# Raw centroids turned first, inverse norms spread by a product, first loads on one queue, and a new order of the early work

## The chip, the cores and the metric

The kernel runs on one core of a Trainium2 chip. The metric is the device time of one execution in microseconds. The kernel before takes 226.15 us as the median of three runs (226.10 to 226.18). Five engines work side by side, each through its own list of instructions in order: TensorE (PE, with its weight loads as PEld), VectorE (DVE), ScalarE (ACT), GpSimd (POOL) and SyncE (SP), which here only issues transfers. An instruction that waits holds up all that stands behind it on its engine.

## The reference, cut to what matters

```python
c_n = centroids / (norm(centroids, axis=-1) + 1e-06)        # 8 heads x 16 centroids x 64
q_assign = argmax(einsum('bhsd,hcd->bhsc', q_n, c_n), axis=-1)   # same for k
mask = q_assign[:, :, :, None] == k_assign[:, :, None, :]
scores = where(mask, scale * q @ k.T, -1e9)                  # 4 batches x 8 heads x 768 x 768
attn = softmax(scores);  x = attn @ v                        # then (3072, 512)
h = x @ w_in                                                 # 512 -> 1024
ln = layer_norm(h * softmax(h)) * g_ln
out = ln @ w_out                                             # 1024 -> 512
```

Each query row and key row gets the centroid of its head with the largest product. The mask lets a query see only keys with the same centroid. Only the direction of a centroid row counts, so each of the 128 rows (8 heads by 16) is divided by its norm.

## The kernel before, in words

A batch and two heads make a pair; there are 16 pairs. For each pair the kernel loads q and k (`raw`), turns them so that the 64 features lie on partitions (`xt`), multiplies them by the centroids on PE (`csc`, name `cl`), turns the result back on DVE (`cst`, `tb`), takes the maximum (`mx`), marks it (`oh`), turns the marks (`oht`, `ot`) and places them (`pl`) as 16 more rows under the cast features (`ca`) in the tile `qk`. One PE product over 80 or 96 rows (`S`, tile `sps`) then gives score and mask together. ACT takes exponentials (`E`, tile `e`), PE multiplies them by v (`V`, tile `ops`), DVE divides (`N`). The second half of the model runs in blocks of 128 rows: product with w_in (`h`), maximum (`hm`), exponential (`ex`), product (`u`), statistics (`bn`, `ag`, `al`), turn (`tu`), product with w_out (`y`), scale (`sc`) and store (`ou`).

The program is written by a weaver: every piece of work has a name, and five strings in `ORDER` say in which order the names stand on each engine. `AWAY` moves single pieces to another engine than their usual one. `add` gives a piece its function and what it needs; the costs there only order the writing of the program. On PE the names `wm` and `fl` stand for idle products on zeros (`idle_p`, line 854), which keep the engine at work until real work arrives. The first pair is done in two halves, one for each head (`halves_of`): q and k of head 0, then of head 1. `tp` turns a half on PE (line 402), `xa` copies it out of PSUM (line 409).

The centroids: SyncE issues their load first (line 841). DVE sums squares (line 877), POOL takes the root (line 880), DVE refines and inverts it (lines 882 to 889) and writes the scaled rows twice side by side (`c_n`, line 890). PE turns them (`cp`, line 899), DVE multiplies by a 0/1 mask `own` into `c_by_two` (`cf`, line 903), which the first five pairs use. Later PE turns them again (`cq`) and DVE writes `c_bd` (`cb`, line 910), which the other pairs use.

Tokens keep PSUM areas apart: `take="m"` and `give="m"` share one bank between `cp`, `cq`, `cl` and `y`.

Of the kernel before, what the change touches and what calls it, by code (L numbers as in the profile page):

```python
# [22 lines left out]
class Weave:  # L23
# [6 lines left out]
        ld4 lv si ld6 lv ld lg lv ld2 lo2 lv lo ld2 lo ld6 li4 tx ld lv ld6 lv tx lv tu ld5 lv ld tx  # L30
        ld tu ld tu ld8 ou ld tu ou ld4 lv ld7 lv ld tu ld4 ou tx ld tu ld4 ou tx ld5 ou ld tu ld2
        lv ld tu ld tx ld4 ou ld3 ou pl ld5 tu lv ld4 lv tu ou tu ld3 lv ou tx ld lv tu ld2 pl ou tx
        ld2 ou pl tu ou lv tx tu pl ou tu2 tx2 tu ou tx2 tu ou tu ou tx tu ou tu ou tu ou6
    """
    ORDER["POOL"] = """
        zo po =ca0.0.0.1.0 ca =pl0.0.0.1.1 pl cv =ca0.1.0.1 =ca0.1.0.0 =pl0.0.1.0.0 pl z
        =pl0.0.1.0.1 ca pl ca =cv0.1.1 =ca0.2.1.1 pl =ca0.2.0.1 pl2 ca2 =ca0.3.1.1 cv =pl0.2.0.0
        =ca0.3.1.0 cv pl =ca0.3.0.1 z pl =cv0.3.1 =ca1.0.0.0 cv =ca1.0.1.0 pl =z4 gs z ca =pl1.0.1.1
        sg ca =pl1.0.0.1 pl2 wi4 =ca1.1.1.0 =cv1.0.1 =ca1.1.0.1 cv =ca1.1.1.1 =at1 =ca1.2.0.1 at ca
        al =pl1.1.1.1 cv =pl1.1.0.0 pl bl pl ca z =ca1.2.1.1 al at ca cv =pl1.2.1.1 =pl1.2.0.0 al  # L40
        =pl1.2.0.1 pl =ca2.0.1.0 bl cv =ca1.3.0.1 at =cv1.3.1 =ca1.3.1.0 ca al =pl1.3.1.1 =pl1.3.0.0
        pl cv bl pl =cv2.1.0 ca =pl2.0.0.0 pl =at5 pl2 at al =ca2.0.1.1 =ca2.1.0.0 =pl2.1.0.1
        =ca2.1.1.1 ca cv al =ca2.3.0.0 bl cv =pl2.1.1.1 =ca2.2.0.1 =ca2.1.1.0 =pl2.1.0.0 =ca2.2.0.0
        pl bl =ca2.3.1.1 at2 al =ca2.2.1.0 cv ca cv pl =ca2.3.1.0 pl at pl =pl2.3.1.1 =pl2.3.1.0 ca
        pl at pl al =ca3.0.0.0 ca =ca3.0.1.0 bl ca =cv2.3.1 al =ca3.1.1.1 cv =pl3.0.0.0 =pl3.0.1.1
        pl bl =ca3.2.0.1 al ca =cv3.0.1 cv pl at2 ca al =pl3.1.1.1 =ca3.3.0.0 =ca3.2.0.0 =cv3.1.1
        =pl3.2.0.1 al =pl3.1.0.1 pl =ca3.2.1.0 =cv3.2.1 pl =ca3.3.0.1 cv ca cv at =ca3.3.1.0 pl cv
        al ca at =pl3.3.0.1 at =pl3.3.1.1 al pl ca =at17 at al2 at al at al =at21 at al2 =at22 at
        al3 at al
    """  # L50
    ORDER["PE"] = """
        wm fl2 tp fl2 tp fl8 cp tp fl7 cl tp fl11 cl fl16 tp S tp S cq S2 tp S tp2 S V S tp V S tp
        cl V S tp2 S V S2 V tp S V S gt tp S2 cl S2 V2 S V S tp S V S V S tp S V S cl S2 V S V3 S2
        tp2 S V S V2 S tp S V S2 cl S V S V2 S2 V S su S3 V4 S3 su S V S2 V S V2 S2 me S2 V2 S2 V2
        S2 cl S2 V S V S V2 h S3 h S h S h S V S V3 S2 h V h V S2 V S h S V S h S2 V S V h S V h S3
        V3 y2 S y S h2 S h V y S2 V2 S h cl V S2 h V h S3 h S V y S y3 V S2 V S V h V S h S V S V S
        y S h y S3 V y S V S V2 S y S V2 S2 cl h V S h S2 h V S V S2 y V S V2 S2 y S2 y2 S V h V S V
        S2 V2 S V cl S2 V2 S cl S V2 S2 y S V S V S y S V S y S V S2 y S V S V2 h V S h S h2 S y4 S
        V S h2 S V S h2 S V S V cl V h S h S V S2 cl S h S h V S2 V h S V2 h y2 S2 y2 S2 V2 S h S2 h
# [129 lines left out]
def kernel(  # L189
# [461 lines left out]
    def values(n, j):  # L651
# [4 lines left out]
        if s == 0:  # L656
            opss[g] = ps_o.tile([P, 6, VS], F32, name="ops")
# [638 lines left out]
```

## Time and profile before

| | us |
|---|---|
| median of 3 runs | 226.15 (226.10 to 226.18) |
| profiled execution, its own time | 227.3 |
| span of that execution (first to last instruction) | 225.3 |
| PE busy | 219.2 (97%) |
| DVE busy | 200.3 (89%) |
| ACT busy | 191.3 (85%) |
| POOL busy | 127.7 (57%) |

The profiled execution is 2.0 us longer than its span and 1.15 us longer than the median. Busy time of PE counts the time in which a product is in flight. The granted clock of PE is 1.0 throughout, yet idle products of one shape take different times early and late, which the chain of waits shows. In the forty equal slices of the span PE is at 9 tenths in all but the first and the last.

### The profile page before, as it was taken

How to read it: one execution, taken by the hardware profiler on the slowest of the kernel's cores; microseconds unless marked ns; L12 is line 12 of the kernel's file. 1: busy time of each engine (PE TensorE's matmuls, PEld its weight loads, DVE VectorE, ACT ScalarE, POOL GpSimd, SP SyncE). 2: the span in 40 equal slices, each digit the busy share in tenths (PEclk: the TensorE clock that was granted, in tenths of full speed). 3: DMA queues.
4: the chain of work that ended last, by engine and by line, in shares of the span. 5: the costliest groups of instructions: out<-in, count | busy, mean ns of one | idle time of the engine just before them, and what ended most of it. 6: DMA issues, size and time to landing. Idle time of an engine off the chain costs nothing.

```text
span 225.3 us, 6745 instructions
## 1 busy us (share of the span) xinstructions
PE 219.2 (97%) x2501; PEld 146.8 (65%) x2501; DVE 200.3 (89%) x359; ACT 191.3 (85%) x366; POOL 127.7 (57%) x246
## 2 busy tenths in 40 slices
PE   8999999999999999999999999999999999999993
PEld 8877864666666767666566656676666677665452
DVE  2799997899999999999999899898998996879982
ACT  3399988999979999998989979899989899964353
POOL 3379985942385597289995670957965102122341
PEclk9999999999999999999999999999999999999999
DMA  5999994289999999799997998789771724659522
GB/s 182 366 370 354 196 243 191 47 163 220 187 179 153 213 179 169 148 161 175 184 219 155 147 215 149 180 170 162 175 166 58 93 28 116 90 155 177 166 83 103
DMA packets 117327, 38.80 MB, mean 172 GB/s; under 512 B 105640, under 2 KB 112816, under 8 KB 117296
## 3 DMA queue, kind: packets, MB, share of 16 engines
q1 hardware_dynamic: 117008, 38.06, 79.0%
q8 instruction: 19, 0.31, 0.6%
q10 hardware_dynamic: 288, 0.33, 0.4%
q14 instruction: 12, 0.10, 0.2%
HBM read 23.11 MB, written 6.29 MB: 130 GB/s over the span
## 4 chain that ended last, share of the span: by engine, by line
PE 80%; DVE 10%; ACT 2%; POOL 2%; issue 2%; DMA 1%; SPq 1%; DVEq 0%; ACTq 0%; POOLq 0%
PE sps L637 23%; PE hreg L746 16%; PE yps L810 16%; PE ops L660 12%; PE hreg L402 3%; PE csc L476 3%; PE idle_p L854 3%; DVE xt L427 2%; ACT e L643 2%; PE csc L471 1%; DMA raw<-in_q_dram 1%; DVE nmax L752 1%; DVE y L827 1%; DVE oh L510 1%; PE hreg L609 1%
## 5 line engine op out<-in xcount | busy, mean ns | idle before, releaser
L643 ACT ACTIVATE e<-sps 128x512 bf16<-128x512 f32 x288 | 150.6, 610 | 10.5 <-PE sps L637 8.6
L637 PE MATMUL sps<-qk 80*128 80x256 bf16 (+3 forms) x648 | 98.9, 260 | 0.3
L637 PEld LDWEIGHTS <-qk 80*128 80x128 bf16 (+1 forms) x648 | 52.1, 97 | 32.0 <-issue 8.6
L660 PEld LDWEIGHTS <-e 128*128 128x128 bf16 x1152 | 52.5, 97 | 16.0 <-issue 4.0
L660 PE MATMUL ops<-v,e 128*128 128x65 bf16 x1152 | 58.7, 193 | 0.5 <-DVE x L685 0.3
L746 PE MATMUL hreg<-w_in_sb,xT 128*128 128x512 bf16 x192 | 54.4, 379 | 0.0
L810 PE MATMUL yps<-w_out_c,uT 128*128 128x512 bf16 x184 | 49.9, 379 | 0.3 <-DVE y L827 0.3
L765 DVE TENSOR_TENSOR u<-e_sb,hreg 128x1024 bf16<-128x1024 bf16 (+1 forms) x25 | 29.1, 1166 | 5.0 <-ACT e_sb L758 4.9
L758 ACT ACTIVATE e_sb<-hreg,nmax 128x1024 bf16<-128x1024 f32 x24 | 26.8, 1118 | 6.7 <-DVE nmax L752 6.5
L776 DVE BATCH_NORM_STATS2 bs<-u 128x6 f32<-128x512 bf16 x48 | 31.6, 676 | 0.3
L550 POOL COPY qk<-oht 32x384 f32<-32x384 f32 x40 | 20.6, 515 | 18.8 <-DVE oht L523 14.9
L752 DVE TENSOR_REDUCE nmax<-hreg 128x1 f32<-128x1024 f32 x24 | 28.9, 1203 | 1.3 <-PE hreg L746 1.1
L456 POOL CAST qk<-xt 64x768 bf16<-64x768 f32 (+1 forms) x31 | 25.5, 823 | 6.9 <-DVE xt L409 3.0
L458 POOL TENSOR_SCALAR qk<-xt 64x768 bf16<-64x768 f32 (+1 forms) x28 | 23.4, 836 | 4.0 <-PE yps L810 2.3
L810 PEld LDWEIGHTS <-uT 128*128 128x128 bf16 x200 | 17.8, 97 | 11.5 <-ACT uT L742 0.8
L746 PEld LDWEIGHTS <-xT 128*128 128x128 bf16 x192 | 16.5, 97 | 8.1 <-issue 0.6
L792 POOL TENSOR_SCALAR esq<-es,mv 128x1 f32<-128x1 f32 x24 | 8.1, 339 | 22.6 <-DVE mv L780 22.0
L427 DVE STREAM_TRANSPOSE xt<-raw 128x768 f32<-128x768 f32 x22 | 20.9, 959 | 0.0
L685 DVE TENSOR_TENSOR x<-ops,den 128x256 bf16<-128x256 f32 (+1 forms) x39 | 18.9, 486 | 1.3
L786 POOL TENSOR_SCALAR es<-esum 128x1 f32<-128x1 f32 x24 | 5.6, 239 | 23.3 <-ACT e_sb L758 14.9
L568 POOL CAST v<-vf 128x384 bf16<-128x384 f32 x27 | 14.3, 532 | 7.7 <-DMA vf<-in_v_dram 4.7
L795 POOL TENSOR_TENSOR alpha<-esq,halves 128x1 f32<-128x1 f32 x24 | 13.4, 560 | 2.0
(82 smaller groups left out, 186.6 us busy)
## 6 DMA issues: line engine op xcount, KB each, us to landing
vf<-in_v_dram SPq DMA_DIRECT2D x16, 384.0 KB, 4.4
out_dram<-y SPq DMA_DIRECT2D x23, 256.0 KB, 2.8
raw<-in_q_dram SPq DMA_DIRECT2D x44, 96.0 KB, 3.2
raw<-in_k_dram SPq DMA_DIRECT2D x44, 96.0 KB, 3.4
w_g<-in_moe_w_out_dram SPq DMA_DIRECT2D x4, 512.0 KB, 8.0
w_st<-in_moe_w_in_dram SPq DMA_DIRECT2D x4, 512.0 KB, 6.9
raw<-in_q_dram SPq DMA_DIRECT2D x4, 384.0 KB, 7.2
raw<-in_k_dram SPq DMA_DIRECT2D x4, 384.0 KB, 7.8
```

The costliest lines, as they stand in the source:

```text
L427: nc.vector.transpose(xt[:], raws[b, p, i][:].rearrange("p j c -> p (j c)"))
L456: VEC[e].tensor_copy(dst, src)
L458: VEC[e].tensor_scalar(dst, src, scalar1=inv_C, scalar2=1.0, op0=Alu.mult, op1=Alu.mult)
L637: nc.tensor.matmul(sps_[n, k][:, c0:c0 + w], side(b, h // 2, 1, h % 2, keys)[r], side(b, h // 2, 0, h % 2, slice(s0 * P, s0 * P + w))[r])
L643: nc.scalar.activation(es[n, k][:, :w], sps_[n, k][:, :w], Act.Exp, scale=exp_scale, bias=-exp_scale)
L660: nc.tensor.matmul(opss[g][:, s, :VW], es[n, k][:, c0:c0 + P], v1[slot(b, h // 2)][:, h % 2, kt, :VW], start=(kt == 0), stop=(kt == n_t - 1))
L746: uses(nc.tensor.matmul(hreg[:, at(f, f2)[1], :], xTs[f][:, dc, :], w_in_sb[:, dc, f2 * FF2:(f2 + 1) * FF2], start=(dc == 0), stop=(dc == ...
L752: uses(nc.vector.tensor_reduce(ff[f, "nmax"][:], pair_of(f), axis=AXY, op=Alu.max, negate=True), *both(f))
L758: uses(nc.scalar.activation(ff[f, "e"][:], pair_of(f), Act.Exp, bias=ff[f, "nmax"][:], accum_out=ff[f, "esum"][:]), *both(f))
L765: uses(nc.vector.tensor_tensor(ff[f, "u"][:, at_], ff[f, "e"][:, at_], pair_of(f)[:, at_], op=Alu.mult), *banks)
L776: nc.vector.bn_stats(ff[f, "bs"][:, f2, :], ff[f, "u"][:, f2, :])
L810: ins = nc.tensor.matmul(dst, ff[f, "uT"][:, at(f, f2)[0] * (n_fc // 2) + c, :], w_out_c[:, fc, cols], start=(fc == chunks[0]), stop=(fc = ...
```

## The change

The load of the centroids is issued twice, by SyncE and by ACT, into the two halves of `c_two`. PE turns these raw rows as its first real work (`cp`), ACT copies the turned rows to SBUF (`ct`, tile `c_t`). Squares, root and inverse go on meanwhile; the formula for the norm is written with one step of another kind (`c_s1`). When the inverse norms `c_inv` are there, PE multiplies them, repeated over 128 columns, by the identity (`ci`): this puts the inverse of each centroid in its column on all rows of PSUM. DVE then multiplies turned rows and inverses straight into place, in six small products: `cg` for the first pair, `cf` for the other heads of `c_by_two`, `cb` for `c_bd`. POOL clears those two tiles first and no longer makes `own`. The PSUM bank is that of `ops`, so the first `V` now needs `cf` and `cb`, and `cq` is gone.

The first load of q, which ACT issued, is issued by SyncE. In the first pair ACT copies all four turned halves (`xa`) and places one of the marks (`pl0.0.0.1.0`). The five orders are written anew from end to end, with 53 idle products in place of 72.

```diff
@@ -27,67 +27,64 @@
     ORDER["PE"] = """
-        wm fl2 tp fl2 tp fl8 cp tp fl7 cl tp fl11 cl fl16 tp S tp S cq S2 tp S tp2 S V S tp V S tp
+        wm cp fl10 tp2 ci tp fl2 cl tp fl9 cl fl14 tp S2 tp S tp S2 tp2 S2 tp cl tp S V2 S2 tp S tp
...
     AWAY.update(dict.fromkeys("""
-        ca0.0.0.0.0 ca0.0.0.1.1 ca1.3.1.1 sc23.0 tu22.1 tu23.1 xa0.0.1.0 xa0.2.1.0 xa0.2.1.1
-        xa0.3.0.0
+        ca0.0.0.0.0 ca0.0.0.1.1 ca1.3.1.1 sc23.0 tu22.1 tu23.1 pl0.0.0.1.0 xa0.0.0.1 xa0.0.1.0
+        xa0.2.1.0 xa0.2.1.1 xa0.3.0.0
     """.split(), "ACT"))
...
-            opss[g] = ps_o.tile([P, 6, VS], F32, name="ops")
+            opss[g] = ps_o.tile([P, 6, VS], F32, name="ops", tag="ops")
...
-    c_all = const.tile([P, D], F32, name="c_all")
-    nc.sync.dma_start(out=c_all[:], in_=centroids.rearrange("h c d -> (h c) d"))
+    c_two = const.tile([P, 2, D], F32, name="c_two")
+    for x, e in enumerate((nc.sync, nc.scalar)):
+        e.dma_start(out=c_two[:, x, :], in_=centroids.rearrange("h c d -> (h c) d"))
     for hh in range(2):
         for i in range(2):
-            load_head(0, 0, i, hh, nc.sync if i or hh else nc.scalar)
+            load_head(0, 0, i, hh, nc.sync)
...
-    own = const.tile([P, 2 * NC_], F32, name="own")
-    for hh in range(2):
-        for x in range(2):
-            nc.gpsimd.memset(own[hh * D:(hh + 1) * D, x * NC_:(x + 1) * NC_], float(hh == x))
+    nc.gpsimd.memset(c_by_two, 0.0)
+    nc.gpsimd.memset(c_bd[:], 0.0)
...
     c_r0 = const.tile([P, 1], F32, name="c_r0")
     nc.vector.reciprocal(c_r0[:], c_s0[:])
-    nc.vector.scalar_tensor_tensor(out=c_r0[:], in0=c_r0[:], scalar=c_nsq[:], in1=c_s0[:],
+    c_s1 = const.tile([P, 1], F32, name="c_s1")
+    nc.vector.tensor_scalar(c_s1[:], c_s0[:], scalar1=2e-6, scalar2=None, op0=Alu.add)
+    c_norm = const.tile([P, 1], F32, name="c_norm")
+    nc.vector.scalar_tensor_tensor(out=c_norm[:], in0=c_r0[:], scalar=c_nsq[:], in1=c_s1[:],
                                    op0=Alu.mult, op1=Alu.add)
-    c_norm = const.tile([P, 1], F32, name="c_norm")
-    nc.vector.tensor_scalar(c_norm[:], c_r0[:], scalar1=0.5, scalar2=1e-6,
-                            op0=Alu.mult, op1=Alu.add)
     c_inv = const.tile([P, 1], F32, name="c_inv")
     nc.vector.reciprocal(c_inv[:], c_norm[:])
-    nc.vector.tensor_scalar(c_n[:], c_all[:].unsqueeze(1).to_broadcast([P, 2, D]),
-                            scalar1=c_inv[:], scalar2=None, op0=Alu.mult)
-    add("wm", "PE", 3.55, -1000, lambda e: [idle(P) for _ in range(26)])
+    add("wm", "PE", 3.55, -1000, lambda e: [idle(P) for _ in range(18)])
...
+    def turn_centroids():
+        cs["t"] = ps_o.tile([P, 2, P], F32, name="cps", tag="ops")
+        nc.tensor.transpose(cs["t"][:, 0, :], c_two[:].rearrange("p a d -> p (a d)"), ident_f[:])
+
+    c_t = const.tile([P, P], F32, name="c_t")
+
+    def spread_inverse():
+
+        nc.tensor.matmul(cs["t"][:, 1, :], c_inv[:].to_broadcast([P, P]), ident_f[:])
+
+    def keep_blocks(dst, lo, hi, step):
+
+        for x in range(2):
+            r = slice(x * D, (x + 1) * D)
+            src = [y.rearrange("p (h c) -> p h c", c=NC_) for y in (c_t[r], cs["t"][r, 1, :])]
+            hs = slice(lo + (x if step == 2 else 0), hi, step)
+            nc.vector.tensor_tensor(dst[r, :, x * NC_:(x + 1) * NC_], src[0][:, hs], src[1][:, hs],
+                                    op=Alu.mult)
+
+    add("wa", "ACT", 2.75, -1000, lambda e: None)
+    add("cp", "PE", 0.42, 0, lambda e: turn_centroids(), [])
+    add("ct", "ACT", 0.3, -600, lambda e: nc.scalar.copy(c_t[:], cs["t"][:, 0, :]), ["cp", "wa"])
+    add("ci", "PE", 0.42, 0, lambda e: spread_inverse(), ["cn", "cp"])
+    add("cg", "DVE", 0.25, -500, lambda e: keep_blocks(c_by_two[:, 0:2], 0, 2, 1), ["ci", "ct"])
+    add("cf", "DVE", 0.3, -490, lambda e: keep_blocks(c_by_two[:, 2:H], 2, H, 1), ["ci", "ct"])
+    add("cb", "DVE", 0.3, -480, lambda e: keep_blocks(c_bd[:], 0, H, 2), ["ci", "ct"])
...
+                if n == 0:
+                    nd += ["cf", "cb"]
                 add(f"V{n}.{j}", "PE", 0.193, t_to[n] - 1 + j + 0.5,
                     (lambda e, n=n, j=j: values(n, j)), nd, [prev] if prev else [])
```

Three places show what moved. The first is the head of DVE's list, from the norms to the first marks. Before, with line numbers of the kernel before:

```order
L882 RECIPROCAL c_r_153<-c_s_151 128x1
L883 SCALAR_TENSOR_TENSOR c_r_153<-c_r_153,c_nsq,c_s_151 128x1
L886 TENSOR_SCALAR c_norm<-c_r_153 128x1
L889 RECIPROCAL c_inv<-c_norm 128x1
L890 TENSOR_SCALAR c_n<-c_all,c_inv 128x128
L458 TENSOR_SCALAR qk_99<-xt 64x3x128
L903 TENSOR_TENSOR w_out_c<-cps,own 128x256
L409 COPY xt<-hreg 128x384
L485 STREAM_TRANSPOSE cst<-csc 128x192
```

And now (`c_by_two` lies inside the tile `w_out_c`):

```order
L881 RECIPROCAL c_r_151<-c_s_149 128x1
L883 TENSOR_SCALAR c_s_153<-c_s_149 128x1
L885 SCALAR_TENSOR_TENSOR c_norm<-c_r_151,c_nsq,c_s_153 128x1
L888 RECIPROCAL c_inv<-c_norm 128x1
L910 TENSOR_TENSOR w_out_c<-c_t,cps 64x2x16 x2
L455 TENSOR_SCALAR qk_99<-xt 64x3x128
L482 STREAM_TRANSPOSE cst<-csc 128x192
```

The scaling of the rows and the copy of a turned half are gone from here, and the product over 128x256 became two over 64x2x16, ahead of the cast.

The second place is DVE's list behind the first half, up to `c_bd`. Before:

```order
L409 COPY xt<-hreg 128x384
L498 TENSOR_REDUCE mx<-cst 128x12
L910 TENSOR_TENSOR c_bd<-cps,own 128x128
L568 CAST v_0_105<-vf 128x6x64
L504 TENSOR_TENSOR w_out_c<-cst,mx 128x6x2x16
```

And now, from the cast of v on:

```order
L567 CAST v_0_105<-vf 128x6x64
L482 STREAM_TRANSPOSE cst<-csc 128x192
L406 COPY xt<-hreg 128x384
L495 TENSOR_REDUCE mx<-cst 128x12
L910 TENSOR_TENSOR w_out_c<-c_t,cps 64x6x16 x2
L406 COPY xt<-hreg 128x384 x2
L501 TENSOR_TENSOR w_out_c<-cst,mx 128x6x2x16
L517 STREAM_TRANSPOSE oht<-w_out_c 128x384
L910 TENSOR_TENSOR c_bd<-c_t,cps 64x4x16 x2
```

`c_bd` stood ahead of the marks of the second half and of three copies; it now stands behind the marks, their turn and five copies (one each after the marks and after the turn).

The third place is the end of DVE's list, the last block. Before:

```order
L740 COPY uT<-utp 128x512
L776 BN_STATS bs<-u 128x6
L765 TENSOR_TENSOR u<-e_sb,hreg 128x512
L780 BN_AGGR mv<-bs 128x2
```

And now:

```order
L775 BN_STATS bs<-u 128x6
L739 COPY uT<-utp 128x512
L764 TENSOR_TENSOR u<-e_sb,hreg 128x512 x2
L779 BN_AGGR mv<-bs 128x2
```

The statistics changed places with the copy, and the two halves of `u` follow each other with nothing between.

More of the change, by code (lines that the diff above doesn't have):

```diff
@@ L38 @@
[L38 to L43, printed above, removed]
@@ L1037 @@
                 e = ("DVE", "POOL")[j % 2] if half else "POOL" if apart(b, p) else "SP"
-                costs = ({"DVE": 0.3, "POOL": 0.41} if half else
+                costs = ({"DVE": 0.3, "POOL": 0.41, "ACT": 0.46} if half else
                          {"POOL": 0.76, "DVE": 0.46} if apart(b, p) else
```

136 lines of the change are left out of this document (63 added, 73 removed).

## The prediction

> **What bounds the kernel now.** I read the page first, then the table of waits, then the chain of waits over the first 16 us.
>
> ```profile
> span 225.3 us, 6745 instructions
> ...
> PE 219.2 (97%) x2501; PEld 146.8 (65%) x2501; DVE 200.3 (89%) x359; ACT 191.3 (85%) x366; POOL 127.7 (57%) x246
> ...
> PE idle_p L854 <- DVE halves L858: 1.0, 1, 1.0
> PE hreg L810 <- ACT uT L742: 0.5, 1, 0.5
> ```
>
> PE is busy for 97% of the span. Its largest waits (us in total, times, longest) are the start, 1.0, and one of 0.5 near the end. So PE is the bound: what it does in order between start and end adds up to the time. Real products can't be dropped by this change. What can go is time that PE spends on idle products (`idle_p`), and waits. The idle products lie before the first score product, so I read the chain there (start, us, what):
>
> ```profile
> 0.97 3.17 PE idle_p L854 x28
> 4.14 0.64 PE hreg L402 x3
> 4.78 0.21 PE idle_p L854 x2
> ...
> 5.63 0.85 PE idle_p L854 x8
> 6.49 0.21 PE cps L899
> ...
> 7.11 0.39 PE idle_p L854 x7
> 7.50 0.46 PE csc L471 x8
> 7.96 0.48 PE hreg L402 x3
> 8.44 0.61 PE idle_p L854 x11
> ...
> 9.53 1.00 PE idle_p L854 x16
> 10.53 0.33 PE hreg L402 x3
> 10.86 0.35 PE sps L637 x2
> ...
> 11.54 0.22 PE sps L637 x2
> 11.76 0.11 PE cps L899
> ...
> 13.74 0.18 PE ops L660 x6
> ```
>
> The first score product starts at 10.86; until then 72 idle products take 6.2 us. An idle product costs 0.113 us in the first 28 and 0.056 in the seven at 7.11; three turns cost 0.64 early and 0.33 late. PE speeds up to double between 6.5 and 7.1, though the page's row of the granted clock shows full speed everywhere.
>
> **The front, step by step.** The timeline rows that carry it:
>
> ```profile
> 0.72 0.40 SPq L841 DMA_DIRECT2D c_all<-in_centroids_dram  x1
> 3.14 0.23 DVE L877 CUSTOM_DVE_ANT_0 c_n<-c_all 128x64 f32<-128x64 f32 x1 [1.82 <-DMA c_all<-in_centroids_dram]
> 4.70 0.16 DVE L889 RECIPROCAL c_inv<-c_norm 128x1 f32<-128x1 f32 x1
> 6.74 0.42 DVE L903 TENSOR_TENSOR w_out_c<-cps,own 128x256 f32<-128x256 f32 x1
> 12.10 0.28 DVE L910 TENSOR_TENSOR c_bd<-cps,own 128x128 f32<-128x128 f32 x1
> 8.48 0.48 ACT L409 COPY xt<-hreg 128x384 f32<-128x384 f32 x1 [2.33 <-PE hreg L402]
> 8.85 1.07 ACT L454 ACTIVATE qk<-xt 64x384 bf16<-64x384 f32 x2
> 9.30 0.58 DVE L520 STREAM_TRANSPOSE oht<-w_out_c 128x384 bf16<-128x384 bf16 x1
> 9.92 0.58 DVE L532 COPY qk<-oht 16x192 f32<-16x192 f32 x2
> 10.03 0.73 POOL L532 COPY qk<-oht 16x192 f32<-16x192 f32 x2 [1.76 <-DVE oht L520]
> raw<-in_q_dram ACTq DMA_DIRECT2D x1, 192.0 KB, 2.7
> ```
>
> Centroids land at about 3.1 (DVE starts on them at 3.14). ACT issues its copy at the same moment as it issued q, and that larger load landed 2.7 us after its issue, at 3.4: so both halves of `c_two` are there between 3.1 and 3.4; I take 3.2. The 18 idle products end at 0.97 + 18 x 0.113 = 3.0, so PE waits 0.2 us, turns the raw rows (0.21) until 3.4 and does ten idle products (1.06, by the eight at 5.63) until 4.5. Moving q's first load to SP puts each load behind the centroids back by one issue (0.40 in the row at 0.72; with the gap I take 0.5): q lands at 3.9, k, one issue behind it, about 4.4, ahead of the two groups of turns at 4.5 and 5.15 (0.64 each, end 5.8). They are hidden by these idle products; without them the delay would cost its 0.5.
>
> The norms take the same four small DVE steps behind the same root, so `c_inv` is ready at 4.86 as before; it is off the path by 0.9 us. The spreading product `ci` has no row. From below: a turn of the same shape, 0.21 early. From above: twice that, 0.42, since the four cluster products, also in float, stand as x8 in the chain, two passes each. I take 0.42: end 6.2. The scaling of the rows (L890, 0.29) and the wait behind the eight idle products are gone.
>
> `cg` is two products over 64x32. The rows at 6.74 and 12.10 (256 and 128 columns, 0.42 and 0.28) give 0.14 plus 0.0011 a column, so 0.18 each: DVE is done at 6.25 + 0.36 = 6.6, against 7.16 before. The turn of q's second half (0.64) ends at 6.85 and two idle products at 7.0, where `cl` starts, not at 7.50. ACT's copies are ready: 5.2 + 0.48 and 5.85 + 0.48. So **0.5 us** is gained here, between 0.3 (if the centroids land at 3.4) and 0.7 (`ci` at 0.21).
>
> From `cl` to the first score it took 10.86 - 7.50 = 3.36. Its last step was two marks on POOL, until 10.76. One of them moves to ACT. DVE's two end at 10.50; ACT starts its one behind its casts (8.85 to 9.92 before, shifted like the rest) and I price it by the copy at 8.48, 0.48, so 10.56. That is 0.2 less, in both bounds between nothing and 0.26. First score: 7.0 + 3.36 - 0.2 = **10.16**. PE's own list agrees: 7.0 + 0.46 + 0.48 + nine idle (0.50) + 0.46 + the wait for ACT's fourth copy (0.1) + 14 idle (0.84) + 0.33 = 10.17. So 0.7 us early.
>
> **Up to the first V.** Now something is given back: the PSUM bank is shared, and the first `V` waits for `cb`, far down DVE's list.
>
> ```profile
> 10.90 0.56 DVE L409 COPY xt<-hreg 128x384 f32<-128x384 f32 x1
> 11.37 0.34 DVE L498 TENSOR_REDUCE mx<-cst 128x12 f32<-128x192 f32 x1
> 11.63 0.55 DVE L409 COPY xt<-hreg 128x384 f32<-128x384 f32 x1
> 12.29 0.35 DVE L568 CAST v<-vf 128x384 bf16<-128x384 f32 x1
> 12.56 0.98 DVE L504 TENSOR_TENSOR w_out_c<-cst,mx 128x192 bf16<-128x192 f32 x1
> 13.47 0.55 DVE L409 COPY xt<-hreg 128x384 f32<-128x384 f32 x1
> 13.93 0.56 DVE L520 STREAM_TRANSPOSE oht<-w_out_c 128x384 bf16<-128x384 bf16 x1
> 15.47 0.85 PE L471 MATMUL csc<-xt,w_out_c 128*32 128x384 f32 x8
> ```
>
> From start to start a copy takes 0.47 (10.90 to 11.37), the maximum 0.26, the cast of v 0.27, the marks 0.91; their turn is 0.56 long. From 10.0, where DVE's marks now end (10.50 less 0.5), the list up to `cb` is: cast 0.27, `tb` 0.34 (by the full maximum over the same 192 columns), five copies 2.35, maximum 0.26, `cf` two at 0.25 (96 columns each), marks 0.91, turn 0.56, `cb` two at 0.21: 5.6, so 15.6, and V at 15.7. The same steps at full durations, with `cf` and `cb` paid twice at 0.42 and 0.28, give 0.35 + 0.34 + five times 0.55 + 0.34 + 0.84 + 0.98 + 0.56 + 0.56 = 6.7, so 16.7 and V at 16.8.
>
> PE, from 10.16, has eight `S` (0.22 each), six turns (0.33) and the first `cl` of a whole pair (0.78) before that V: 4.5, so 14.7, plus the wait of `cl` for the fourth copy of its own pair (14.2 on DVE by the same list, against 13.4 on PE): about 15.55. So V costs PE 0.15 of waiting. Queued behind V are more scores and turns, and with them ACT. Where does this stand against before? At 15.5 before, PE had done eight `S`, seven turns, twelve products of V (0.36) and the second turn of the centroids (0.11), and was starting that `cl`. Now, at 15.7, it has `cl` done (0.78) and no V: 0.78 - 0.36 - 0.11 less the 0.2 of the clock is **0.1 us ahead** on PE. But DVE, which before turned the marks at 13.93 with the fourth copy still behind them, now has that copy done at 14.2, half a us and more ahead, and the waits that follow are PE's for DVE. So I carry 0.1 (PE's own) to 0.7 (the first score's), and take 0.4, the middle.
>
> **The middle and the end.** Behind 16 us the instructions are the same in number on each engine, in another order. PE's longest wait behind the start is 0.5 in all, so re-cutting them moves tenths of a us in either direction; I take nothing, with 0.8 each way. At the end one thing can be read:
>
> ```profile
> 217.71 0.69 DVE L765 TENSOR_TENSOR u<-e_sb,hreg 128x512 bf16<-128x512 bf16 x1 [0.62 <-ACT e_sb L758]
> ```
>
> DVE's two halves of `u` now follow each other, without the small statistic between (its instruction costs about 0.1 of DVE's time, less than the 0.16 of the smallest DVE row above); the statistics put ahead of the copy fit into the 0.62 that DVE waited. That is **0.1 us**. Nothing else in the end is shorter, since the last turn can't start before `u`.
>
> **Sum.** 0.4 + 0.1 = 0.5 us. The sum is made against the profiled execution: span 225.3 to 224.8, its time 227.3 to 226.8. That execution lies 1.15 above the median, and I take the same step off the median: 226.15 - 0.5 = **225.65 us**.
>
> **The rivals.**
>
> *The lead is lost behind 16 us* (226.1). For it: DVE is busy 89% and ACT 85%. A DVE list in another order that costs PE five waits of 0.1 is enough. Against it: PE's waits now are short, and all engines have the lead, not PE alone.
>
> *V waits for `c_bd`*, the case on the other side. At the upper price V starts at 16.8, 1.1 us later than I take; the lead of 0.4 turns into 0.7 behind, and with the 0.1 of the end that is 226.75. It decides from 16.1 on, where the lead is spent. For it: the marks took 0.98 at 12.56, nearly three times what the maximum over as many columns took (0.34), so DVE can be held up there. Against it: steps on DVE overlap in every row above, and I have the 0.91 in.
>
> *PE stays slow for longer.* It doubled its speed 5.5 us after its start; now it stands still for 0.2 at 3.0 and has 19 idle products fewer. If the doubling comes only with the first score, at 10.16 and not at 6.6, the work of the 3.6 us between goes at half speed, so half of it, 1.8, is late: 226.15 - 0.5 + 1.8 = 227.45. Against it: the stop is short, and idle products and turns fill the rest.
> The Trainium skill's page "TensorE: Matmul & The Clock Gate" (Part 1: The HAM clock gate) says the clock opens after one busy window of about 3.4 us, and that this window runs freely and doesn't begin anew with the kernel. By that rule a short stop could cost a whole window, or nothing, by where it falls; the rows above (0.113, then 0.056) agree with its two speeds, and no row here shows a window.
>
> *The middle gains too.* The weight sums (line 609) wait in PE's list for POOL, which now has the spreading of g some places earlier:
>
> ```profile
> 34.67 1.06 PE L609 MATMUL hreg<-w_g,w_out_c 128*32 128x512 f32 x8 [0.25 <-POOL v L1261]
> ```
>
> That wait of 0.25 and twice as much elsewhere would make it 225.65 - 0.7 = 224.95.
>
> **Chances and range.** Lead kept 0.56, lead lost 0.18, V waits 0.10, PE slow 0.06, middle gains 0.10. Bounds of "lead kept": 0.1 + 0.1 less half the 0.8 of the middle, and 0.7 + 0.1 plus that half, thus 224.95 to 226.35. The range of 8 in 10 runs from 224.7 to 226.7: it takes in the lost lead and the middle's gain and leaves out the two slow cases for the most part. A measurement of this kernel can tell 0.2%, 0.45 us, from no change, and 225.65 lies just beyond that. So lead kept gives 0.31 to faster, 0.23 to no change and 0.02 to slower; lead lost 0.04, 0.11 and 0.03; V 0.03 to no change and 0.07 to slower; PE slow 0.06 to slower; the middle 0.10 to faster. Sums: faster 0.45, same 0.37, slower 0.18.
>
> **What will show it.** First score at about 10.2 and `cl` at 7.0 in the timeline. A row for `ci` of 0.2 to 0.42. The start of the first V: at 15.7 the lead is 0.4; beyond 16.1 the second rival's price is paid. Idle products at 0.056 from about 7. The last turn of `u` a tenth earlier, measured back from the end. The forecast is wrong if the first score isn't before 10.6, or if it is and the span is still 225.1 or more: then the middle took it.

## The result, and the profile after

The changed kernel takes 228.33 us (median of 16 runs, 226.74 to 230.08); the kernel before, beside it, 226.12 (16 runs). The ratio is **1.0104**, 95% interval 1.0075 to 1.0132: 1% slower, where 0.2% faster was forecast, and outside the range of 224.7 to 226.7. In a second comparison it is 1.0056 (1.0034 to 1.0077). One execution each of e2 (442.56 us), e6 (231.32, the one that was profiled) and e8 (231.18) was far slower than the others of its kernel and stands in no ratio and no median below.

The executions of the change differ more among themselves in this comparison: their spans run from 224.2 to 227.6, median 225.85 (in the second comparison from 224.6 to 225.3), where those of the kernel before, over five comparisons, run from 222.9 to 225.1 with medians of 223.9 to 224.0. The profiled execution of the change has a span of 224.5, so it is one of its shortest. The page and the table of waits of it (us in total, times, longest):

```profile
span 224.5 us, 6721 instructions
...
PE 217.5 (97%) x2483; PEld 145.3 (65%) x2483; DVE 198.9 (89%) x361; ACT 192.0 (86%) x369; POOL 126.6 (56%) x243
...
PE hreg L399 <- DMA raw<-in_q_dram: 0.7, 1, 0.7
PE hreg L399 <- DMA raw<-in_k_dram: 0.5, 1, 0.5
...
DVE xt L424 <- DMA raw<-in_k_dram: 0.4, 1, 0.4
```

PE is busy 1.7 us less than in the profile before (219.2), and the time is longer all the same. Three waits for loads are new: PE's two in the front, and DVE's, which comes 109 us in. Its chain of waits (start, us, what) from the first instruction on, the pieces that answer to those shown of before:

```profile
2.10 0.43 SPq L381
...
2.58 4.87 DMA raw<-in_k_dram
...
7.49 0.55 PE hreg L399 x3
...
10.35 0.45 PE sps L636 x4
...
13.59 1.15 PE csc L468 x8
...
15.43 0.37 PE ops L659 x12
```

Before, this chain began with idle products; now it begins with SyncE's row of issues, whose fourth load, k of head 1, lands 4.87 us after its issue. The first score starts at 10.35, the first V at 15.43. The same kernel, profiled once more:

```profile
0.97 2.10 PE idle_p L854 x18
3.07 0.36 PE cps L896
3.43 1.07 PE idle_p L854 x10
4.50 1.28 PE hreg L399 x6
5.78 0.43 PE cps L902 x2
...
6.79 0.51 PE csc L468 x8
...
10.10 0.44 PE sps L636 x4
...
11.70 0.26 DVE w_out_c L910
...
11.98 0.57 DVE xt L406
...
12.60 0.55 PE hreg L399 x3
...
15.76 0.37 PE ops L659 x12
```

Here the loads are in time, and the steps of the forecast stand one for one: centroids turned at 3.07 (forecast 3.2), `ci` 0.43 long (0.42), `cl` at 6.79 (7.0), first score at 10.10 (10.16), first V at 15.76 (15.7). Between the first score and the first V the chain runs over DVE once: a product of `cf` at 11.70, the copy behind it, and at 12.60 a turn that has waited for that copy. This execution has a span of 224.7, 0.8 above the median of the kernel before. Step for step the front did what was forecast, and the time went elsewhere.

### The profile page after: what moved, and what is told of

Read it like the earlier page. It is cut to its first block, busy times and chain, and to the rows that moved or that the text cites. A ratio compares the mean times of both kernels' runs of the same rounds, so it can differ in the third digit from the quotient of the medians.

```text
span 224.5 us, 6721 instructions
## 1 busy us (share of the span) xinstructions
PE 217.5 (97%) x2483; PEld 145.3 (65%) x2483; DVE 198.9 (89%) x361; ACT 192.0 (86%) x369; POOL 126.6 (56%) x243
## 4 chain that ended last, share of the span: by engine, by line
PE 77%; DMA 6%; DVE 5%; SPq 4%; POOL 3%; ACT 1%; issue 1%; ACTq 0%; POOLq 0%; DVEq 0%
PE sps L636 24%; PE yps L809 15%; PE hreg L745 15%; PE ops L659 13%; DMA raw<-in_k_dram 6%; PE csc L473 3%; PE hreg L399 2%; SPq L418 2%; PE csc L468 2%; DVE u L764 1%; POOL qk L455 1%; POOL qk L549 1%; DVE xt L424 1%; DVE bs L775 1%; PE hreg L809 1%
## 5 line engine op out<-in xcount | busy, mean ns | idle before, releaser
L659 PE MATMUL ops<-v,e 128*128 128x65 bf16 x1152 | 57.1, 193 | 0.0
L809 PEld LDWEIGHTS <-uT 128*128 128x128 bf16 x200 | 18.3, 97 | 11.2 <-issue 0.5
L567 POOL CAST v<-vf 128x384 bf16<-128x384 f32 x27 | 13.5, 502 | 4.9 <-DMA vf<-in_v_dram 4.1
L824 ACT ACTIVATE y<-yps,alpha 128x512 f32<-128x512 f32 x13 | 8.9, 688 | 6.5 <-PE yps L809 5.6
```

Source lines behind the costliest of these rows:

```text
L659: nc.tensor.matmul(opss[g][:, s, :VW], es[n, k][:, c0:c0 + P], v1[slot(b, h // 2)][:, h % 2, kt, :VW], start=(kt == 0), stop=(kt == n_t - 1))
L809: ins = nc.tensor.matmul(dst, ff[f, "uT"][:, at(f, f2)[0] * (n_fc // 2) + c, :], w_out_c[:, fc, cols], start=(fc == chunks[0]), stop=(fc = ...
```

## The experiments

Every kernel below is timed against the kernel before on the same chip. To see where time is won or lost, one landmark is read in each trace: the starts of ACT's 288 exponentials (`e<-sps`), which come in every kernel in the same number. Written are the 1st, 25th and 49th, and the median over the executions of the span and of the time outside it (own time less span). The landmarks are those of one profiled execution for each kernel. Two profiles of one kernel differ at the 1st by 0.44 (the kernel before) and 0.55 (e11 and e18), and keep that difference up to the 25th; so differences of landmarks are read between the 1st and the 25th or 49th, not at the 1st alone.

| kernel | ratio (95%) | 1st | 25th | 49th | span | outside |
|---|---|---|---|---|---|---|
| before, the profile that the forecast used | | 11.25 | 25.61 | 40.07 | | |
| before, profiled again (e5) | | 10.81 | 25.17 | 39.85 | 223.9 | 1.9 to 2.4 |
| change | 1.0104 (1.0075 to 1.0132) | 10.61 | 26.06 | 40.10 | 225.85 | 2.50 |
| e1 change again | 1.0056 (1.0034 to 1.0077) | 10.36 | 26.41 | 40.66 | 224.95 | 2.49 |
| e2 new front, old rest | 1.0043 (1.0024 to 1.0062) | 10.30 | 25.66 | 40.45 | 224.6 | 2.46 |
| e3 old front, new rest | 1.0086 (1.0059 to 1.0113) | 11.21 | 27.35 | 41.87 | 225.7 | 2.41 |
| e4 idle products filled in | 1.0067 (1.0045 to 1.0090) | 10.59 | 26.27 | 40.31 | 224.9 | 2.48 |
| e6 change, q on ACT | 1.0117 (1.0083 to 1.0151) | 12.27 | 27.90 | 42.16 | 226.1 | 2.48 |
| e7 q on SyncE alone | 1.0010 (0.9986 to 1.0034) | 10.80 | 25.30 | 39.98 | 224.2 | 1.92 |
| e8 new centroids alone | 1.0109 (1.0077 to 1.0140) | 11.87 | 27.17 | 41.64 | 225.9 | 2.37 |
| e9 e8 with one load | 1.0059 (1.0040 to 1.0078) | 10.36 | 25.66 | 40.12 | 224.45 | 2.46 |
| e10 e8, products on POOL | 1.0061 (1.0035 to 1.0087) | 11.16 | 25.27 | 39.95 | 225.0 | 2.01 |
| e11 e8 with both | 0.9987 (0.9973 to 1.0000) | 11.07 | 25.18 | 39.86 | 223.6 | 2.00 |
| e18 the same again | 0.9985 (0.9965 to 1.0005) | 11.62 | 25.73 | 40.20 | 224.0 | 2.02 |
| e14 second load alone | 1.0049 (1.0019 to 1.0080) | 11.42 | 25.79 | 40.26 | 224.85 | 2.36 |
| e15 change with one load | 1.0061 (1.0040 to 1.0082) | 9.87 | 25.90 | 39.95 | 225.0 | 2.49 |
| e16 change, products on POOL | 1.0016 (0.9997 to 1.0035) | 10.61 | 26.02 | 40.07 | 224.5 | 2.04 |
| e12 change with both | 1.0027 (1.0005 to 1.0049) | 10.52 | 25.94 | 39.99 | 224.5 | 1.95 |
| e17 e12 and one k load ahead | 0.9998 (0.9979 to 1.0017) | 10.17 | 25.59 | 39.64 | 224.15 | 2.02 |
| e13 e12's front, old rest | 0.9996 (0.9975 to 1.0018) | 10.12 | 24.57 | 39.66 | 224.2 | 2.02 |

### Front or rest? (e1 to e4)

e1 is the change unchanged. e2 keeps its code and its order up to the second V and takes the order of the kernel before behind that; e3 is the reverse, with the old code. e4 fills PE's shorter front again:

```diff
-        wm cp fl10 tp2 ci tp fl2 cl tp fl9 cl fl14 tp S2 tp S tp S2 tp2 S2 tp cl tp S V2 S2 tp S V
+        wm cp fl10 tp2 ci fl8 tp fl2 cl fl7 tp fl9 cl fl14 tp S2 tp S tp S2 tp2 S2 tp cl tp S V2 S2 tp S V
```

> The changed kernel unaltered. Its profiled execution was 226.97 us, its median 228.33 with single executions up to 230.08, so one profile does not show what costs the time. Theory C (clock): PE waits 0.7 and 0.5 us for first loads in the front, and in many executions it then works at half speed for longer; then spans of 226 to 227 us go with idle products of 0.11 us and turns of 0.21 still behind 7 us, up to 1.8 us lost there, and nothing behind 16 us. Theory L (loads): q and k of the second head land later than 5.8 and 7.45 in those executions; then PE waits 2 us and more in the front at full speed. Theory M (middle): the new order behind 16 us costs the time, at a place that moves from one execution to the next; then the front is over at 16 us as in the first profile and a later wait is long.

> The changed kernel up to the second V product (about 16 us), with the changed centroids and loads; behind that the remaining work of every engine in the order of the kernel before. Theories C and L: as slow as the changed kernel, 228.3 (227.8 to 228.8), with the same spread of 3 us. Theory M: the 2.2 us are gone, 225.5 to 226.3, and the spread is that of the kernel before, under 2 us.

> The kernel before up to the second V product (centroids, loads and all 72 idle products as before); behind that the remaining work in the order of the changed kernel. Theory M: slow, 228 to 229, with the wide spread. Theories C and L: 225.8 to 226.5, like the kernel before.

> The changed kernel with 15 more idle products on PE where it waited for loads in the first profile: 8 behind the spreading product, 7 behind the first cluster product. Theory C: PE doesn't stand still, so it is at full speed by 7 us in every execution and the median falls by most of the 2.2 us, to 226.0 to 226.8. Theory L: no better, 228.1 to 229, since late loads are waited for anyway. Theory M: unchanged, 228 to 228.7.

Each half is slower than the kernel before by itself, by 0.43% and 0.86%, and together they are not slower than the worse one. So neither half alone holds the whole cause, and e2, at 227.08, fits none of its theories. e3 has to be read with care. From the 1st to the 25th exponential it takes 16.14 us where the kernel before takes 14.36 in both profiles, and from the 25th to the 49th as much as that one (14.52; 14.46 and 14.68). What it has lost by the 49th it lost right behind the seam of an old front and a new rest that were not made for each other, so e3 doesn't show what the new rest costs behind its own front; e12 and e13 come nearer to that. Fifteen idle products more change nothing that can be told (1.0067 against 1.0056), so PE's pauses in the front are not seen to cost.

### Which part of the front? (e5 to e8)

e5 is the kernel before unchanged. e6 puts q's first load on ACT in the change; e7 puts it on SyncE in the kernel before (the same line, the other way). e8 puts only the new centroid code into the kernel before: its loads, idle products and orders stay, `ci` stands where `cp` stood, `cg` where `cf` did, `cf` and `cb` together where `cb` did.

```diff
-            load_head(0, 0, i, hh, nc.sync if i or hh else nc.scalar)
+            load_head(0, 0, i, hh, nc.sync)
```

> The kernel before, unaltered, for a second profile: the one I predicted from had a span of 225.3 us and a time of 227.3, while single executions since then have spans of 223.2 to 225.1. Theory B (base): the profile I started from was a long execution, and its extra 1.4 us lie where the new order was to gain; then this profile has a span near 223.9 and its landmarks (exponentials 24 to 36, at 25.6 and 32.9 us before) come up to 1 us earlier. Theory P (profile is fair): span 225 again.

> The changed kernel with q's first load issued by ACT again, behind ACT's half of the centroids; the other loads move up one issue on SyncE. Theory L (late first loads cost time): 0.3 to 0.5 us less than the changed kernel, whose median beside these runs was 227.4. Theory M (the middle decides): within 0.3 us of it.

> The kernel before with only the one line of the loads changed: q's first load issued by SyncE, all loads behind it half a us later. Theory L: slower than before by 0.3 to 0.5 us, 226.5 to 226.7. Theory M: 226.0 to 226.4, as before, since 10 idle products and more stand between.

> The kernel before with the new centroids alone: two loads of raw rows, turned behind the first 26 idle products, spread at the place of the old turn, six products on DVE at the places of the old two; loads, the 72 idle products and the rest of the order as before. The clusters of the first half then wait for nothing new. If the new centroids cost nothing by themselves: 226.0 to 226.4. Theory D (DVE is the bound behind the front): the 0.3 us that DVE pays more for the products (0.36 + 0.50 + 0.42 against 0.42 + 0.28 + 0.29) show in part, 226.3 to 226.6.

The change of q's queue alone costs nothing that can be told (e7), although PE waited 0.6 and 0.2 us there for loads of the second half. e6 went against its expectation: with q back on ACT the change is slower still; q, now behind ACT's load of the centroids, lands at 5.13, where it landed at 4.04 in e1. The new centroid code alone costs everything: +1.09%, 2.5 us, where 226.6 us at most was expected. e5 shows something else, in its chain:

```profile
0.98 3.17 PE idle_p L854 x28
4.14 0.64 PE hreg L402 x3
4.78 0.21 PE idle_p L854 x2
5.00 0.44 PE hreg L402 x3
...
10.42 0.35 PE sps L637 x2
...
13.30 0.18 PE ops L660 x6
...
15.10 0.78 PE csc L471 x8
```

PE comes to full speed during the turns at 5.00 (0.44, where the profile of the forecast still had 0.85 for eight idle products at 5.63). The first score of the kernel before is at 10.42, not at 10.86. The profile that the forecast started from was a long execution (span 225.3, against a median of 223.9 and no other above 225.1).

In e8's chain, where the second us is lost:

```profile
1.17 3.55 DMA raw<-in_q_dram
...
4.77 0.90 PE hreg L504 x3
...
13.47 0.22 DVE c_bd L1015
...
13.73 0.36 DVE v L672
14.09 0.89 DVE w_out_c L606
...
15.02 0.57 DVE xt L511
...
15.63 0.55 PE hreg L504 x3
...
17.11 0.78 PE csc L573 x8
```

q lands 3.55 us after its issue and PE turns it at 4.77, not at 4.14. Then the chain runs over DVE: the products of `c_bd`, v's cast, the marks, the copy for which PE's turn at 15.63 has waited. The first `cl` of a whole pair starts at 17.11, in e5 at 15.10.

### The two costs apart (e9, e10, e11, e18, e14)

e9: one load, and ACT writes the second half of `c_two` from the first. e10: ACT copies the spread inverses to SBUF (`cj`), and POOL makes the four later products, so V and PSUM wait for ACT's copy only. e11 and e18: both. e14: the kernel before with a second load of the centroids that nothing reads.

```diff
-    for x, e in enumerate((nc.sync, nc.scalar)):
-        e.dma_start(out=c_two[:, x, :], in_=centroids.rearrange("h c d -> (h c) d"))
+    nc.sync.dma_start(out=c_two[:, 0, :], in_=centroids.rearrange("h c d -> (h c) d"))
...
+    add("cw", "ACT", 0.3, -700, lambda e: nc.scalar.copy(c_two[:, 1, :], c_two[:, 0, :]), ["wa"])
```

```diff
-    add("cf", "DVE", 0.3, -490, lambda e: keep_blocks(c_by_two[:, 2:H], 2, H, 1), ["ci", "ct"])
-    add("cb", "DVE", 0.3, -480, lambda e: keep_blocks(c_bd[:], 0, H, 2), ["ci", "ct"])
+    add("cj", "ACT", 0.3, -550, lambda e: nc.scalar.copy(c_i[:], cs["t"][:, 1, :]), ["ci"])
+    add("cf", "POOL", 0.6, -490, lambda e: keep_blocks(c_by_two[:, 2:H], 2, H, 1, e, c_i), ["cj", "ct"])
+    add("cb", "POOL", 0.6, -480, lambda e: keep_blocks(c_bd[:], 0, H, 2, e, c_i), ["cj", "ct"])
...
-                    nd += ["cf", "cb"]
+                    nd += ["cg", "cj"]
```

> The new centroids alone in the old order (+1.09%, 2.4 us), but the centroids are loaded once, by SyncE, and ACT copies the 64 columns into the other half of c_two at about 3.2 us, behind the 26 idle products' cover; q's first load is again ACT's first issue. Theory load: the doubled load costs the front (q landed 3.6 us after its issue instead of 2.6, PE waited 0.4 for it and ran slow longer; the first exponential came at 11.87 instead of 10.81), and that lag is carried to the end: here q lands after 2.7, the first exponential comes at about 11.0 (the turn of the centroids and the spreading product still cost 0.2), and the time falls by 0.8 to 1.2, to about 227.3 (+0.5 to +0.7%). Theory DVE: the front's lag is absorbed by DVE's list anyway; the first exponential moves the same way, but the time stays at +0.9% or more (228.0 or more).

> The new centroids alone in the old order, loads doubled as there, but ACT copies the spread inverses to SBUF (128x128, about 0.27) and POOL, which is idle between 9.1 and 10.6 us, makes the four later products; DVE keeps only the two of cg, and V needs only ACT's copy. Theory DVE: the four products on DVE (0.96 us in two rows, against 0.28 for the one they replaced there) and what V and the turns wait for them cost the second us between 12 and 16 us: the copy that follows the marks starts about 0.7 earlier than 15.02, the 24th exponential about 0.7 to 1.0 earlier than 27.2, the time falls by 0.7 to 1.2, to 227.3 (+0.5%). Theory load: the time stays within 0.3 of 228.4, since the front's lag of 1.05 remains and is what counts. If POOL's four products take more than 0.4 each, they hold up POOL's marks at 10.6 and the first score comes later.

> Both edits: one load of the centroids, and the four later products on POOL behind ACT's copy. If the two costs are apart and add up, 2.4 less 1.0 less 0.9: about 226.4 (+0.2%, between no change and +0.4%), first exponential at about 11.0, 24th within 0.4 of the kernel before's 25.2. If one cause hides the other, no better than the better of the two (+0.5%). If neither is the cause, still +0.9% or more.

> The old order with the new centroids, one load and the later products on POOL, unchanged from its first run (0.9987, interval 0.9973 to 1.0). If it is truly faster, again 0.998 to 0.9995; if the first was chance, 0.9995 to 1.0015.

> The kernel before with nothing changed but a second load of the centroids, issued by ACT ahead of q into a tile that nothing reads. Theory load: a second small load ahead of q delays q's landing (3.6 us after its issue rather than 2.6 to 2.7, and the issue itself 0.45 later) and lets PE wait at its first turn and stay slow longer: first exponential 0.4 to 1.0 later, +0.3 to +0.5% (226.7 to 227.2), with executions spread over 2 to 3 us rather than 1.5. Rival: the second load costs only because the turn of the centroids waits for it; then within 0.1% of the kernel before.

Each mend takes half a per cent off e8, and both together take it all: 1.0109, 1.0059, 1.0061, 0.9987. In the old order both theories hold, each for its half, and together they give more than the expected +0.2%.

*The products.* e9 and e11 differ in the products alone, and so do e8 and e10. From the 1st to the 25th exponential e8 and e9 take 15.30 us each, and e10, e11 and e18 14.11 each; the kernel before takes 14.36. So DVE's products cost 1.19 us there, and 0.97 is left of it at the 49th in both pairs. The medians of the spans differ by 0.85 and 0.9. In the rows of e11's timeline (start, us, engine, line) POOL does them in a gap:

```profile
7.59 0.50 POOL L558 CAST qk<-xt 64x384 bf16<-64x384 f32 x1 [1.44 <-DVE xt L511]
8.06 0.83 POOL L1016 TENSOR_TENSOR w_out_c<-c_t,c_i 64x96 f32<-64x96 f32 x2
8.94 0.71 POOL L1016 TENSOR_TENSOR c_bd<-c_t,c_i 64x64 f32<-64x64 f32 x2
9.85 0.73 POOL L640 COPY qk<-oht 16x192 f32<-16x192 f32 x2 [0.20 <-DVE oht L622]
```

They take longer there (1.54 us) than on DVE in the change:

```profile
11.12 0.51 DVE L910 TENSOR_TENSOR w_out_c<-c_t,cps 64x96 f32<-64x96 f32 x2
...
14.71 0.43 DVE L910 TENSOR_TENSOR c_bd<-c_t,cps 64x64 f32<-64x64 f32 x2
```

and hold nothing up: behind them POOL still waits 0.20 us for DVE's turn of the marks. A lead at the first exponential doesn't make up for the products on DVE: e9's is 0.71 ahead of e11's, its 25th 0.48 behind. The lead as such is kept, though: against e8, which has the same products, e9 is 1.51 ahead at the 1st, 1.51 at the 25th and 1.52 at the 49th.

*The second load.* e14 changes no instruction on PE, DVE or POOL, and is 0.49% slower (0.19 to 0.80). Its chain and its table of waits:

```profile
0.72 0.40 ACTq L843
...
1.15 3.79 DMA raw<-in_q_dram
...
5.08 0.53 PE hreg L402 x3
```

```profile
PE hreg L402 <- DMA raw<-in_q_dram: 0.9, 1, 0.9
```

q is issued 0.43 later, and lands 3.8 us after its issue where it was 2.7: at 4.94 instead of 3.4. The rows show the delay and PE's wait for it, but not how they cost the 0.49%: this execution has a span of 224.0, below e14's median of 224.85, and is only 0.1 longer than e5's. The spread fits a cost that isn't the same each time: e14's executions lie 3.1 us apart (226.04 to 229.12), e10's 2.9 and e8's 2.0, those of e9 and e11, with one load, 1.4 and 1.5. In the change, with two loads, it was 3.3 in the one comparison and 0.7 in the other.

### The same two in the change, and the new order (e15, e16, e12, e13, e17)

e15: the change with one load. e16: the change with the products on POOL. e12: both, with q's first load on ACT again. e13: e12 up to the second V, the order of the kernel before behind it. e17: e12 with one place of SyncE's order changed, so that the last two quarters of a k tile are issued ahead of a turn of x and of a store:

```diff
-        ld5 tu ld8 tu ld4 ou ld ou tu ld3 lv ld4 lv ld3 ou tu lv ld3 ou ld2 tx ld tu ld4 tx ld ou ld
+        ld5 tu ld8 tu ld4 ou ld ou tu ld3 lv ld4 lv ld3 ou tu lv ld3 ou ld2 tx ld tu ld6 tx ou
         tu lv ou ld tx ld2 tu ld14 lv ld tu ou ld2 pl ld4 tu lv ou tu ld ou ld2 lv ld tx tu lv ld2
```

> The change with one load of the centroids and ACT's copy of the 64 columns (22 idle products ahead of their turn, 6 behind it); q's first load stays second in SyncE's queue, the products stay on DVE. Theory load, as in the old order: 0.5% less than the change (+0.56% beside it earlier), so within 0.2% of the kernel before, and the executions closer together. If DVE's list hides it: still +0.5% or more.

> The change with ACT copying the inverses and POOL making the four later products; both loads of the centroids stay. Theory DVE, as in the old order: 0.5% less than the change, so about +0.1%; the 0.45 us outside the span also falls (2.5 to 2.0), as in the other two kernels with these products on POOL. If the new orders have room for them on DVE: still +0.5%.

> The whole change with its orders, but the centroids loaded once and copied by ACT, q's first load back on ACT, the four later products on POOL behind ACT's copy of the inverses, 22 idle products ahead of the centroids' turn and 6 behind it (53 as before). Theory front: what the change loses is in the doubled load and DVE's products; with both mended its front is 0.3 to 0.5 earlier than the kernel before's (first exponential at 10.3 to 10.5) and the time is 225.6 or less (-0.1 to -0.3%). Theory orders: the new orders behind 16 us lose by themselves (the kernel before's front with the new rest took +0.86%): then the time stays at +0.4% or more, about 227, whatever the front does.

> The change with both mends (one load, later products on POOL), front of the new order up to the second V, and behind it the order of the kernel before. Theory orders: the new order behind 16 us costs the whole rest (226.54 against 225.56 for the old order with the same mends; its profile shows 2.1 us lost around the 108th exponential behind a wait of 1.1 for a turned cluster product), so here 225.2 to 225.6, -0.2 to -0.35%. Theory front: the new front itself sets the engines wrongly for what follows; then 226.2 or more (no better than +0.1%).

> The change with both mends, and the last two quarters of one k tile (the eighth load of the third batch) issued ahead of the turn of x and of the store that stood before them in SyncE's queue, about 1.9 us earlier for the last. Theory late load: the wait of 0.4 to 1.5 us at 108.5 on DVE goes in every execution; the slower half of the executions joins the faster: about 226.0, +0.0 to +0.1% (0.3 to 0.5 less than the change with both mends), all within 1 us. Rival: the wait only takes the place of another, or the delayed turn of x is waited for instead; then as before, +0.2 to +0.3%, with two groups.

One load alone mends nothing here (1.0061): the first exponential is then the earliest of all, 9.87, and by the 25th, 25.90, the lead over the kernel before has become a lag. That expectation missed. In the old order q stands behind the second load on ACT; in the change it is on SyncE, and lands at 3.56 to 4.10 with the second load (five profiles) and at 3.63 without it (e15). The products on POOL take the change from 1.0056 to 1.0016: half of it, 0.45 us, in the span, the other half outside it (2.49 to 2.04). e10 and e11 had shown that second half too; no run explains it. The landmarks agree with the first half: from the 1st to the 25th exponential e1 and e15 take 16.05 and 16.03, and e16, e12 and e17, with POOL's products, 15.41 or 15.42. The change's first profile takes 15.45, so its products didn't cost this in every execution.

e12 is no better than e16, and between its two theories. The profile of one of its longer executions (227.4 us) shows a wait that is left. Chain, and below it a row of DVE's timeline:

```profile
104.38 0.41 SPq L836
...
104.83 5.03 DMA raw<-in_k_dram
```

```profile
109.99 0.98 DVE L424 STREAM_TRANSPOSE xt<-raw 128x768 f32<-128x768 f32 x1 [1.50 <-DMA raw<-in_k_dram]
```

The last quarter of a k tile is issued behind a store (line 836), lands at 109.86, and DVE has stood for 1.5 us; in the change itself this wait is the 0.4 of its table, in e6 1.3, in e3 0.8, in e15 0.5, in e4 0.2, in e1 and e16 none. No kernel with the old order behind 16 us shows it. In e17 those loads are together:

```profile
100.19 2.78 SPq L418 DMA_DIRECT2D raw<-in_k_dram  x4
...
108.07 0.97 DVE L424 STREAM_TRANSPOSE xt<-raw 128x768 f32<-128x768 f32 x1
```

The wait is gone and e17 is at 0.9998. Its interval overlaps that of e12 a little (0.9979 to 1.0017, 1.0005 to 1.0049), so the 0.29% between them is shown by the row and only made likely by the time. e17's executions still lie 1.5 us apart, as those of the kernel before do; that the late load makes two groups of them did not hold.

e13 holds its lead of 0.6 over the kernel before up to the 25th exponential (24.57 against 25.17) and has 0.2 left at the 49th; its span (224.2) is no shorter, and its time lies between its two theories. Where e13 takes 14.45 from the 1st to the 25th exponential, the new rest takes 15.4 (e12, e16, e17); from the 25th to the 49th it is 15.09 against 14.05, so the new rest gives most of that back. Fully mended, the new front and the new orders end where the kernel before ends. The best of all is the old order with the new centroids, one load and POOL's products (e11, e18): 0.9987 and 0.9985, each interval reaching to 1.0 or just beyond, so a gain of 0.1 to 0.15% is likely and not certain.

## Why the prediction was wrong

**The chip's own steps held.** Eighteen idle products to 3.07, `ci` at 0.39 and 0.43, `cl` at 6.44 and 6.79, first score at 10.35 and 10.10, first V at 15.43 and 15.76, the four later products at 0.94 (0.92 in the sum). The end too: the first half of `u` starts 7.46 before the end of the span, where it was 7.59, so the forecast 0.1:

```profile
217.04 1.28 DVE L764 TENSOR_TENSOR u<-e_sb,hreg 128x512 bf16<-128x512 bf16 x2 [0.72 <-ACT e_sb L757]
```

**"Sum made against the profiled execution" failed.** The 0.7 us at the first score were counted from 10.86. Of these 0.44 belonged to that one execution, in which PE came late to full speed; the median that the sum was taken off did not have them. Counted from 10.42 the lead is 0.1 to 0.3. The prediction had seen that its execution was 1.15 us above the median and took the step off the median unchanged. It also took the 2.0 us outside the span as fixed; in the change 2.5 lie there (medians before: 1.9 to 2.4), and why stays open.

**"Hidden by these idle products" held only in part.** That step priced the loads of head 0 (q at 3.9, k at 4.4) and left out those of head 1, which stand third and fourth in SyncE's row. In the first profile they landed at about 5.8 and at 7.45, and PE waited 0.7 and 0.5. These waits are not shown to have cost the change its time: the first score came at 10.35 with them and at 10.10 without, and e7 has such waits and is not slower. The second load of 32 KB was priced by its own landing alone. In the old order, where q stands behind it, it cost 0.49%; in the change, where q doesn't, e15 shows no cost.

**"So I carry 0.4 us" failed.** The lead at the first V was measured by what PE had done in the late execution. In the other profile's timeline the kernel before starts its first whole `cl` at 15.03 and not at 15.47 (15.10 and 15.54 in the chain), so at that V nothing was left. And DVE, which has 0.94 for the four products where the old `cb` took 0.28, is the engine that sets the pace there: in the old order they cost 1.19 us between the 1st and the 25th exponential, in the change 0.6 in e1 and e15, where the forecast had 0.15 of PE's waiting. With the products on POOL the change is at 1.0016 in place of 1.0056, about half of it inside the span. Of the steps that failed, this is the one whose cost is shown in the change itself. The argument that DVE was "half a us and more ahead" compared one copy and not the list.

**"I take nothing, with 0.8 each way" for the middle failed in its sign.** Behind the mended front the new rest gives 1.0027 (e12) and the old rest 0.9996 (e13), so it costs about 0.3%, with intervals that overlap a little. One part of it is seen in the rows, the late quarter of a k tile: the wait is there in e12 and gone in e17 (0.9998). The rule that PE's waits were short before said nothing of a load that moves behind a store. That this wait is the whole of it is not shown, and e1, at 1.0056, has no such wait. Open is also the 0.5% between the two comparisons of the change (1.0104 and 1.0056).

**The rivals.** "V waits for `c_bd`" had the place and the engine (DVE) right and gave 226.75; but V was not late (15.43 and 15.76). What waits is a turn for the copy that DVE makes behind the products, at 12.60 in the change's second profile and at 15.63 in e8. "The lead is lost behind 16 us" happened and was only the start. "PE stays slow longer" is seen in single executions. The one of e6, its longest, has these in its chain:

```profile
8.00 0.80 PE csc L468 x8
8.79 0.83 PE hreg L399 x3
```

In e1 the same products at 6.79 take 0.51 and the turns behind them 0.48. How often the change pays this, the single profiles can't say. Nor does a late clock always lengthen the execution: e11 and e18 are one kernel, eight idle products take 0.85 in e18's timeline at 5.64 and 0.61 in e11's at 5.33, e18's first exponential comes 0.55 later, and both spans are 224.1. The Trainium skill's page "TensorE: Matmul & The Clock Gate" (Part 1: The HAM clock gate) has a window that runs freely; two profiles of the kernel before, which come to full speed during the turns at 5.00 and ahead of the idle products at 7.11 on one list of instructions, agree with that, and no run here shows the window itself. The forecast's own mark of being wrong, a first score before 10.6 with a span of 225.1 or more, is met by the median of the spans in the first comparison (225.85) and just missed in the second (224.95).

## What to carry to other kernels

Compare a step with several executions before taking a lead from one: 0.44 of the 0.7 us forecast at the first score were one execution's late clock. A lead in front doesn't pay for work that is added to the engine that sets the pace behind it, so price a moved step on that engine's list, and give the work to an engine with a gap there even if it takes longer on it. Count each transfer of the queue that a new one goes ahead of, down to the last one that is waited for.

## What was not expected of the hardware

Where ACT issued a load of 32 KB (landing 1.8 to 2.1 us after its issue) ahead of q's 192 KB, q landed 3.4 to 4.0 us after its own issue (e6, e8, e10, e14); where ACT issued q's load first, it landed after 2.6 to 2.7 (nine profiles). The small load ahead is hardly the whole cause. On SyncE the centroids also stand ahead of q in the change, e1, e2, e4, e7, e15 and e16, and q landed after 2.4 to 2.9. In the four late cases k left SyncE within 0.03 us of q, and landed late too, after 3.2 to 3.8, where in the nine profiles it took 2.6 to 2.8. Two large loads that leave at one moment may be what counts; no run parts the two.

The time outside the span differs from kernel to kernel: 2.4 to 2.5 us (medians) in the kernels with the new `cf` and `cb` on DVE, 1.95 to 2.05 in all seven measurements with these on POOL, and either in those with the old code, e3 and e14 at 2.4, e7 at 1.9, and the kernel before, whose executions lay at 1.9 to 2.0 in one comparison and between 1.9 and 2.6 in others. The difference is 0.2% of the time, and its cause stays open.
